# Wide loads, 128-key tiles, planned dates and zero matmuls in a fused attention and MLP kernel

## The chip, the cores and the metric

The kernel runs on one core of one Trainium2 chip. The metric is the device time of one execution in microseconds (us); a median of several executions is given, with the lowest and highest. A profile is one such execution. Its span is from the first to the last recorded instruction. PE is TensorE, PEld its weight loads, ACT ScalarE, DVE VectorE, POOL GpSimd, SP SyncE.

## The reference

Attention over 8 batches of 12 heads, 448 tokens and 64 channels, with root-mean-square normalised q and k, followed by an MLP with a hard swish between its two products.

```python
q, k, v: (8, 12, 448, 64)   g_q, g_k: (64,)   w_in: (768, 2048)   w_out: (2048, 768)

q_n = q / sqrt(mean(q * q, -1) + 1e-6) * g_q          # k_n likewise
attn = softmax(q_n @ k_n.T / sqrt(64))
x = (attn @ v).transpose(0, 2, 1, 3).reshape(8 * 448, 768)
h = x @ w_in
out = (h * clip(h + 3, 0, 6) / 6) @ w_out              # (3584, 768), float32
```

## The kernel before

The work goes by pairs of heads: 6 pairs per batch, 48 in all. A pair of k and q is loaded, squared, reduced, scaled and turned (its channels brought onto the partitions). Scores are then computed with the keys on the partitions, in four tiles of 112 keys, and go through an exponential. The value matmuls follow; v carries a column of ones, which gives the softmax's denominator. The normalised rows are turned again into `xT`, and the MLP of a batch can start when all six pairs of it are in `xT`. The MLP of batch b runs interleaved with the attention of batch b+1, so PE is full once batch 0 is done; before that it has only batch 0's attention to do. The kernel describes all work as steps with durations and due times, and a small greedy planner fixes each engine's order before the program is built.

```python
T = 4; PT = S // T                                   # 112 partitions, 4 tokens in each
def load_g():                                        # four loads of single elements, on ScalarE's queue
    for a in range(2):
        nc.scalar.dma_start(out=gq_t[a * 64:(a + 1) * 64, :], in_=g_q.rearrange("(p o) -> p o", o=1))
        nc.scalar.dma_start(out=gk_t[a * 64:(a + 1) * 64, :], in_=g_k.rearrange("(p o) -> p o", o=1))
# ... cut ...
def score(t0=t0, taken=taken):                       # attend(P): a tile of 112 keys, two heads
    for i, (ps, _, _) in enumerate(taken):
        for a in range(2):
            rows, c0 = slice(a * 64, a * 64 + 64), (t0 + i) * PT
            nc.tensor.matmul(out=ps[:, a, 0:S], lhsT=kp[rows, c0:c0 + 128],
                             rhs=kq[rows, 1, :], start=True, stop=True)
# ... one exponential of 112x896 per tile, then the values:
def values(dst, c0, first):
    for a in range(2):
        for t in range(T):
            nc.tensor.matmul(out=dst[:, a * E1:(a + 1) * E1], lhsT=e[0:PT, t, a, c0:c0 + 128],
                             rhs=va[0:PT, a, t, :], start=(first and a == 0 and t == 0), stop=(t == T - 1))
# ... cut ...
NPE = 10                                             # pairs whose q and k are turned by PE, the rest by DMA
def weights(c, at, load, kept):                      # 8 weight loads, issued by GpSimd between its other work
    kept[c] = add("POOL", 0.9, at, lambda: load(c), gate, xfer=4.4, after=at)
# ... cut ...
with tc.manual_schedule():
    for s in plan.order():
        s.fn(s.eng)
```

Of the kernel before, what the change touches and what calls it, by code (L numbers as in the profile page):

```python
# [15 lines left out]
RELU = mybir.ActivationFunctionType.Relu  # L16
AX_X = mybir.AxisListType.X
PSUM = bass.MemoryType.PSUM

# [13 lines left out]

class Plan:
# [3 lines left out]

    LAT = {"PE": 0.20, "ACT": 0.18, "DVE": 0.15, "POOL": 0.20, "SP": 0.0}
    DMA_LATENCY = 1.7  # L40
    SOFT, HARD = 0.64, 0.425
    AHEAD, HURRY = 0.0, 6.0

    def __init__(self):
        self.steps = []

    def add(self, on, dur, due, fn, *deps, xfer=0.0, after=0.0, lock=False, late=0.0):
        on, f = ({on: dur}, lambda e: fn()) if isinstance(on, str) else (on, fn)
        s = Step(on, due, f, deps, xfer, after, lock, late, len(self.steps))
        self.steps.append(s)  # L50
        return s

    def hard(self, soft, at, todo):

        for t0, t1 in soft:
            if t1 <= at:
                continue
            part = min(todo, max(0.0, t0 - at))
            at, todo = at + part, todo - part
            if todo <= 0:  # L60
                return at
            part = min(todo, (t1 - at) * self.HARD)
            at, todo = at + part / self.HARD, todo - part
            if todo <= 0:
                return at
        return at + todo

    def order(self):
        users = {id(s): [] for s in self.steps}
        left = {}  # L70
        for s in self.steps:
            left[id(s)] = len(s.deps)
            for d in s.deps:
                users[id(d)].append(s)
        free = dict.fromkeys(self.LAT, 0.0)
        port = dma_free = dma_soft = 0.0
        soft = []
# [3 lines left out]
        def release(s):  # L81
            for e in s.on:
                ready[id(s), e] = max([s.after] + [
                    d.end + (0.06 if d.eng == e and not d.xfer else self.LAT[d.eng]) for d in s.deps])
                open_[e].append(s)

# [4 lines left out]
        while len(done) < len(self.steps):  # L91
            best = None
            for e, l in open_.items():
                for s in l:
                    at = max(free[e], ready[id(s), e], port if s.lock and e in ("DVE", "POOL") else 0.0)
                    if best is None or at < best[0]:
                        best = (at, e)
            assert best is not None, "steps wait for each other"
            at, e = best
            near = []  # L100
            for s in open_[e]:
                t = max(at, ready[id(s), e], port if s.lock and e in ("DVE", "POOL") else 0.0)
                if t <= at + self.AHEAD:
                    near.append((s.due + self.HURRY * (t - at), s.n, t, s))
            _, _, at, s = min(near)
# [3 lines left out]
            free[e] = s.end = at + s.on[e]  # L109
            if s.lock and e in ("DVE", "POOL"):  # L110
                port = s.end
            if s.xfer:
                if e == "POOL":
                    at = max(dma_soft, s.end)
                    dma_soft = at + s.xfer / self.SOFT
                    soft.append((at, dma_soft))
                    s.end = dma_soft + self.DMA_LATENCY
                else:
                    dma_free = self.hard(soft, max(dma_free, s.end), s.xfer)
                    s.end = dma_free + self.DMA_LATENCY + s.late  # L120
            done.append(s)
            for u in users[id(s)]:
                left[id(u)] -= 1
                if not left[id(u)]:
                    release(u)
# [3 lines left out]
class Ring:  # L129


    def __init__(self, bufs):
        self.bufs = bufs
        self.used = [[] for _ in bufs]
        self.i = -1

    def take(self):
        self.i += 1
        k = self.i % len(self.bufs)
        before, self.used[k] = self.used[k], []  # L140
        return self.bufs[k], before, self.used[k]
# [3 lines left out]
def kernel(  # L145
# [16 lines left out]
    T = 4  # L162
# [7 lines left out]
    NP = B * NJ  # L170
    assert PT == 112 and S - SM == 64 and D == 64 and NKT == NJ and B % 2 == 0
# [7 lines left out]
    gq_t, gk_t, gp = (const.tile([128, 1], FP32, name=n) for n in ("gq_t", "gk_t", "gp"))  # L179
    mark = const.tile([1, 1], FP32, name="mark")  # L180
    ident = const.tile([128, 128], BF16, name="ident")
    w_in_sb = const.tile([128, NKT, DFF], BF16, name="w_in_sb")
    w_out_sb = const.tile([128, NFT, DM], BF16, name="w_out_sb")

    qk_r = Ring(tiles("qk", 5, [128, 2, 2, T * D], FP32))
    vf_r = Ring(tiles("vf", 5, [128, 2, T * D], FP32))
    sq_r = Ring(tiles("sq", 2, [128, 2, 2, T * D], FP32))
    ssq_r = Ring(tiles("ssq", 4, [128, 4 * T], FP32))
    rs_r = Ring(tiles("rs", 4, [128, 4 * T], FP32))
    qks_r = Ring(tiles("qks", 3, [128, 2, T, 2, D]))  # L190
    kq_r = Ring(tiles("kq", 4, [128, 2, S]))
    kp_r = Ring(tiles("kp", 3, [128, S + 16]))
    va_r = Ring(tiles("va", 5, [128, 2, T, E1]))
    e_r = Ring(tiles("e", 3, [128, T, 2, S]))
    xn_r = Ring(tiles("xn", 3, [128, NS, 2, D]))
    rd_r = Ring(tiles("rd", 3, [128, NS, 2], FP32))
# [6 lines left out]
    X_r = Ring(tiles("X", 1, [128, 512], FP32, psum))  # L203
    R_r = Ring(tiles("R", 1, [128, 512], FP32, psum))
    M_r = Ring(tiles("M", 2, [128, 512], FP32, psum))

    plan = Plan()
    add = plan.add

    NPE = 10  # L210
    GATE, W_IN_AT, W_OUT_AT, W_STEP = 2, 7.0, 35.0, 6.3
    START, FIRST, PAIR = 9.0, 4.1, 2.3
    LEAD = 4
    HURRY = 0.8
# [27 lines left out]
    for P in range(NP):  # L242
        b = P // NJ
        begin.append(begin[-1] + (FIRST if b == 0 else (
            sum(x[3] for x in seq[b]) / NJ + PAIR + (1.1 if (P + 2) < NPE else 0.0))))
    begin += [begin[-1] + 8.0 * (i + 1) for i in range(8)]

# [4 lines left out]
    def load_g():  # L252
        for a in range(2):
            nc.scalar.dma_start(out=gq_t[a * 64:(a + 1) * 64, :], in_=g_q.rearrange("(p o) -> p o", o=1))
            nc.scalar.dma_start(out=gk_t[a * 64:(a + 1) * 64, :], in_=g_k.rearrange("(p o) -> p o", o=1))
# [7 lines left out]
    def make_ones():  # L263
        for t in va_r.bufs:
            nc.gpsimd.memset(t[:, :, :, D:E1], 1.0)
        for t in kp_r.bufs:
            nc.gpsimd.memset(t[:, S:S + 16], 0.0)

    g_load = add("ACT", 2.2, 0, load_g, after=1.5, late=3.0)
    g_make = add("DVE", 0.1, 0, lambda: nc.vector.scalar_tensor_tensor(  # L270
        out=gp[:], in0=gq_t[:], scalar=8.0, in1=gk_t[:], op0=MULT, op1=MULT), g_load, after=7.5)
    id_make = add("POOL", 0.5, 0, make_ident)
    one_make = add("POOL", 0.6, 0, make_ones)

    def load_w_in(c):
        n = DFF // 4
        nc.gpsimd.dma_start(
# [3 lines left out]
    def load_w_out(c):  # L281
        cols, f0 = slice((c // 2) * HALF, (c // 2 + 1) * HALF), (c % 2) * (NFT // 2)
        nc.gpsimd.dma_start(
# [5 lines left out]
    L, V, SC, KQ = {}, {}, {}, {}  # L289

    def heads(src, P):
        b, j = divmod(P, NJ)
        return src[b, 2 * j:2 * j + 2, :, :].rearrange("h (p t) d -> p h (t d)", t=T)

    def loads(P):
        at = begin[P]
        qk, war, use = qk_r.take()
        res = []
# [375 lines left out]
```

## Time and profile before

| kernel before | |
|---|---|
| time | 443.15 us (442.05 to 443.25, 3 runs) |
| span and time of the profiled execution | 438.6 us, 440.47 us |
| first square, first score, first MLP matmul | 8.89, 14.28, 45.48 us |
| PE busy | 410.6 us, 94% |
| exponentials on ScalarE | 166.3 us |

Two lines of the page's groups show what the change goes for. The columns are: source line, engine, operation, out<-in, shapes and count; then busy us and mean ns of one; then the engine's idle time before them and what ended it.

```profile
L421 ACT ACTIVATE e<-S 112x896 bf16<-112x896 f32 x192 | 166.3, 914 | 64.1 <-PE S L416 64.0
L359 POOL CAST va<-vf 112x512 bf16<-112x512 f32 x48 | 31.5, 658 | 10.4 <-DMA vf<-in_v_dram 10.1
```

The exponential takes 914 ns for 896 columns on 112 of 128 partitions.

One caution: the profiled execution of before was a fast one. The time of most others was 442 to 443 us, 2 us above it. Profiles are therefore used to find where time goes, and the medians to say how much.

### The profile page before, as it was taken

Reading aid. Unit: us, or ns where it says so; the run is one execution under the profiler, and the core shown is the slowest. Engines: PE = TensorE matmul, PEld = TensorE weight load, DVE = VectorE, ACT = ScalarE, POOL = GpSimd, SP = SyncE. Lnnn points to the kernel's source line nnn. Section 1 sums busy time; section 2 is a strip of 40 time slices with the busy share of each in tenths; the row PEclk is TensorE's granted clock in tenths of the full one; section 3 lists DMA queues with packets and bytes.
Section 4 is the critical chain, followed back from the end, with each engine's and each line's share of the span. In section 5 each row is a group of like instructions: output and inputs, shape, how many; then the busy total and the mean of one; then the engine's idle time right before and its main releaser. Section 6 shows DMA issues by size and latency. Waiting matters only on the chain.

```text
span 438.6 us, 9205 instructions
## 1 busy us (share of the span) xinstructions
PE 410.6 (94%) x3663; PEld 229.2 (52%) x3682; DVE 246.3 (56%) x417; ACT 249.0 (57%) x425; POOL 240.2 (55%) x230
## 2 busy tenths in 40 slices
PE   0588799999999999999999999999999999999995
PEld 0355455555455565554455565554455555654563
DVE  1998887657674564456555465556564444334421
ACT  3788588657765666367664677357673665123200
POOL 3499988855757567656765657747757510000000
PEclk9999999999999999999999999999999999999999
DMA  8999999877545745674465655684465420220122
GB/s 241 247 265 261 224 214 193 216 197 192 128 121 148 189 113 136 167 214 111 133 156 157 177 135 145 159 214 109 120 161 164 97 56 12 54 81 0 37 72 73
DMA packets 102923, 64.58 MB, mean 147 GB/s; under 512 B 59744, under 2 KB 99424, under 8 KB 102880
## 3 DMA queue, kind: packets, MB, share of 16 engines
q1 hardware_dynamic: 94544, 57.01, 50.6%
q0 software_dynamic: 7296, 6.29, 9.1%
q10 hardware_dynamic: 1040, 0.69, 0.5%
q8 instruction: 29, 0.48, 0.5%
q14 instruction: 14, 0.11, 0.1%
HBM read 45.61 MB, written 11.01 MB: 129 GB/s over the span
## 4 chain that ended last, share of the span: by engine, by line
PE 80%; POOL 5%; DVE 4%; ACT 3%; issue 3%; DMA 3%; SPq 1%; POOLq 0%
PE M L558 27%; PE M L533 25%; PE S L416 9%; PE X L437 8%; PE S L558 4%; PE R L437 2%; PE S L533 2%; DVE ssq L337 1%; ACT e L421 1%; POOL qks L351 1%; PE X L558 1%; POOL sq L322 1%; POOL va L359 1%; DMA gq_t<-in_g_q_dram 1%; POOL sq L329 1%
## 5 line engine op out<-in xcount | busy, mean ns | idle before, releaser
L421 ACT ACTIVATE e<-S 112x896 bf16<-112x896 f32 x192 | 166.3, 914 | 64.1 <-PE S L416 64.0
L533 PE MATMUL M<-xT,w_in_sb 128*128 128x384 bf16 (+1 forms) x679 | 145.1, 349 | 3.7 <-DVE gT L541 2.9
L351 POOL TENSOR_TENSOR qks<-qk,rs 112x512 bf16<-112x512 f32 x87 | 90.5, 1055 | 86.6 <-ACT rs L344 84.7
L558 PE MATMUL M<-w_out_sb,gT 128*128 128x384 bf16 x736 | 131.8, 326 | 0.0
L558 PEld LDWEIGHTS <-gT 128*128 128x128 bf16 x896 | 82.9, 98 | 57.8 <-issue 7.8
L533 PEld LDWEIGHTS <-w_in_sb 128*128 128x128 bf16 x768 | 69.6, 97 | 67.4 <-issue 12.5
L541 DVE SCALAR_TENSOR_TENSOR gT<-t,M 128x384 bf16<-128x384 f32 (+1 forms) x116 | 70.6, 611 | 59.1 <-ACT t L539 58.3
L539 ACT ACTIVATE t<-M 128x384 f32<-128x384 f32 (+1 forms) x116 | 62.6, 540 | 67.0 <-PE M L533 65.5
L437 PEld LDWEIGHTS <-e 112*128 112x128 bf16 x1536 | 65.1, 99 | 31.4 <-issue 16.0
L337 DVE TENSOR_REDUCE ssq<-sq 112x16 f32<-112x1024 f32 (+1 forms) x49 | 58.4, 1193 | 23.3 <-POOL sq L329 12.2
L329 POOL TENSOR_TENSOR sq<-qk 112x1024 f32<-112x1024 f32 x36 | 68.1, 1892 | 0.0
L416 PE MATMUL S<-kq,kp 64*128 64x448 bf16 x384 | 56.6, 364 | 4.1 <-DVE kp L381 1.7
L437 PE MATMUL X<-va,e 112*128 112x65 bf16 x1152 | 58.6, 196 | 0.8 <-ACT e L421 0.6
L566 DVE COPY y<-M 128x384 f32<-128x384 f32 x46 | 25.6, 556 | 59.2 <-PE M L558 59.0
L359 POOL CAST va<-vf 112x512 bf16<-112x512 f32 x48 | 31.5, 658 | 10.4 <-DMA vf<-in_v_dram 10.1
L392 POOL TENSOR_SCALAR kp<-kq,gp 128x448 bf16<-128x448 bf16 x23 | 32.3, 1402 | 5.3 <-DMA kq<-qks 5.2
L463 DVE TENSOR_TENSOR xn<-X,rd 128x384 bf16<-128x384 f32 x48 | 26.8, 558 | 1.6
L416 PEld LDWEIGHTS <-kp 64*128 64x128 bf16 x384 | 12.2, 94 | 27.7 <-issue 18.0
L437 PE MATMUL R<-va,e 112*128 112x65 bf16 x384 | 20.4, 195 | 0.0
L377 PE MATMUL M<-ident,qks 112*128 112x112 bf16 x80 | 7.9, 242 | 13.0 <-DVE qks L351 12.4
L558 PE MATMUL S<-w_out_sb,gT 128*128 128x384 bf16 x112 | 19.5, 326 | 0.0
L462 DVE RECIPROCAL rd<-X 128x6 f32<-128x6 f32 x48 | 9.2, 192 | 15.3 <-PE X L437 15.2
(42 smaller groups left out, 156.2 us busy)
## 6 DMA issues: line engine op xcount, KB each, us to landing
qk<-in_k_dram SPq DMA_DIRECT2D x48, 224.0 KB, 3.3
vf<-in_v_dram SPq DMA_DIRECT2D x48, 224.0 KB, 3.7
qk<-in_q_dram SPq DMA_DIRECT2D x45, 224.0 KB, 3.4
w_in_sb<-in_moe_w_in_dram POOLq DMA_DIRECT2D x4, 768.0 KB, 11.3
w_out_sb<-in_moe_w_out_dram POOLq DMA_DIRECT2D x4, 768.0 KB, 11.9
out_dram<-y SPq DMA_DIRECT2D x8, 336.0 KB, 3.1
out_dram<-y SPq DMA_DIRECT2D x8, 288.0 KB, 3.4
out_dram<-y SPq DMA_DIRECT2D x8, 240.0 KB, 3.2
```

Of the source, the lines that this page charges most:

```text
L329: parts = [add("POOL", 1.93, at - 10, lambda: nc.gpsimd.tensor_tensor(out=sq[0:PT], in0=qk[0:PT], in1=qk[0:PT], op=MULT), *ld, *war, lock= ...
L337: red = add("DVE", 0.6 * n, at - 8 * hurry + 0.5 * i0, lambda i0=i0, i1=i1, cs=cs: nc.vector.tensor_reduce(out=ssq[0:PT, cs], in_=sq[0:PT, ...
L351: sc.append(add(on, 0, at - 6 * hurry, lambda e, i=i, rs4=rs4: engines[e].tensor_tensor(out=qks[0:PT, i].rearrange("p t h d -> p h t d"), ...
L359: vc = add({"POOL": 0.61}, 0, at - 3, lambda e: engines[e].tensor_copy(out=va[0:PT, :, :, 0:D], in_=vf[0:PT].rearrange("p h (t d) -> p h t ...
L392: nc.vector if e == "DVE" else nc.gpsimd).tensor_scalar_mul(
L416: nc.tensor.matmul(out=ps[:, a, 0:S], lhsT=kp[rows, c0:c0 + 128], rhs=kq[rows, 1, :], start=True, stop=True)
L421: x = add("ACT", 0.93, at + step * (t0 + i) / T + 0.2, lambda t=t0 + i, ps=ps: nc.scalar.activation(out=e[0:PT, t], in_=ps[0:PT, :, 0:S], ...
L437: nc.tensor.matmul(out=dst[:, a * E1:(a + 1) * E1], lhsT=e[0:PT, t, a, c0:c0 + 128], rhs=va[0:PT, a, t, :], start=(first and a == 0 and t ...
L533: nc.tensor.matmul(out=m[:, 0:n], lhsT=w_in_sb[:, kt, f * 128:(f + 1) * 128], rhs=X[:, kt, :], start=(kt == 0), stop=(kt == NKT - 1))
L539: r = add("ACT", 0.08 + n / 1200, due + span, lambda: nc.scalar.activation(out=t[:, 0:n], in_=m[:, 0:n], func=RELU, bias=0.5, scale=1.0 / ...
L541: g = add("DVE", 0.12 + n / 960, due + span, lambda: nc.vector.scalar_tensor_tensor(out=G[:, f, :], in0=t[:, 0:n], scalar=1.0, in1=m[:, 0: ...
L558: nc.tensor.matmul(out=m[:, 0:HALF], lhsT=G[:, f, i * 128:(i + 1) * 128], rhs=w_out_sb[:, f, cols], start=(f == 0), stop=(f == NFT - 1))
```

## The change

Its intent: fewer and fuller instructions for attention, an earlier start, and an order of work that was tuned against a finer model of the engines and DMA queues.

1. Keys in three tiles of 128 and a rest of 64, in place of four of 112. The rests of two heads share one matmul (a block-diagonal weight), those of two pairs one exponential.
2. For batches 0 and 1: loads with 7 tokens on each of 128 partitions ("wide"), q, k and x turned by PE, v cast by GpSimd or ScalarE.
3. g in two row loads, turned by PE; k and q are no longer issued by ScalarE.
4. Three tables, by step number: shifts of due dates (`NUDGES`), fixed engines (`ENGINES`), earliest starts (`HOLD`); and a planner with a model of DMA queues and a backward pass.
5. Explicit waits of GpSimd for VectorE, where the plan marks an operation of each as using the port that they share (see the prediction, "What the skill says").
6. Matmuls of zeros where the plan shows PE idle, up to 115 us. They add zero to parts of the accumulators X and S.

The diff at its core (cuts are marked):

```diff
+NUDGES = {9: -3332, 10: -1597, 11: -472, ... cut: 208 entries ...}
+ENGINES = {46: "ACT", 50: "POOL", 55: "POOL", ... cut: 47 entries ...}
+HOLD = {37: 39, 39: 33, 41: 31, 42: 1, ... cut: 149 entries ...}
+    def load_wide(at, tile_, src, P, war, after):
+        return [add("SP", 0.43, at, lambda: nc.sync.dma_start(
+            out=tile_[:, 0:U].rearrange("p t d -> p (t d)"),
+            in_=heads(src, P).rearrange("h (p t) d -> (h p) (t d)", t=U)), *war, xfer=(8, 1950), after=after)]
... cut ...
-            nc.scalar.dma_start(out=gq_t[a * 64:(a + 1) * 64, :], in_=g_q.rearrange("(p o) -> p o", o=1))
-            nc.scalar.dma_start(out=gk_t[a * 64:(a + 1) * 64, :], in_=g_k.rearrange("(p o) -> p o", o=1))
+        return nc.scalar.dma_start(
+            out=grow[:, i].rearrange("o (a p) -> o a p", a=2), in_=(g_q, g_k)[i]... cut ...)
... cut: scores ...
+                    if t < NS:
+                        for a in range(2):
+                            fns.append(... nc.tensor.matmul(
+                                out=ps[:, a, 0:S], lhsT=kp[a * 64:a * 64 + 64, t * 128:(t + 1) * 128],
+                                rhs=rhs[a], start=True, stop=True))
+                    else:
+                        fns.append(... nc.tensor.matmul(
+                            out=ps[:, slot, 0:S], lhsT=kb[:, P % NJ], rhs=rhs[2], start=True, stop=True))
... cut ...
+    order = plan.order()
+    def fill(t0, t1):
+        while t1 - t0 > 0.1:
+            for t, l in reads:                       # l: when the plan has others reading this tile
+                if not any(x - 0.05 < t0 < y + 0.2 for x, y in l):
+                    n = t.shape[-1]
+                    nc.tensor.matmul(out=t, lhsT=zero[:, 0:128], rhs=zero[:, 0:n], start=False, stop=False,
+                                     skip_group_check=True)
+                    t0 += n / 1200 if t0 < COLD else n / 2400 / FILL
+                    break
+            else:
+                t0 += 0.1
     with tc.manual_schedule():
-        for s in plan.order():
-            s.fn(s.eng)
+        for s in order:
+            if s.eng == "PE":
+                if s.start < FILL_TO and s.start - free > 0.3:
+                    fill(free, s.start - 0.1)
+                free = s.end
+            ins = s.fn(s.eng)
+            if ins is not None and s.lock and s.eng in ("DVE", "POOL"):
+                if s.eng == "POOL" and holder is not None:
+                    tc.add_manual_dep(ins.ins, holder.ins.name, ... cut ..., reason="port")
+                holder = ins if s.eng == "DVE" else None
```

## The prediction

> **What bounds the kernel now.** I read the granted clock first (1.000 on the one core, so nothing is throttled), then the busy times, then the slices, then the same per stage, then the waits and the timeline. Busy time of the engines:
>
> ```profile
> PE 410.6 (94%) x3663; PEld 229.2 (52%) x3682; DVE 246.3 (56%) x417; ACT 249.0 (57%) x425; POOL 240.2 (55%) x230
> PE   0588799999999999999999999999999999999995
> DMA  8999999877545745674465655684465420220122
> ```
>
> TensorE is busy nearly throughout, except in the first six or so slices of 11 us. There the DMA row is at its fullest. By stage (busy us of PE, weight loads, VectorE, ScalarE, GpSimd; clock; DMA share; GB/s):
>
> ```profile
> 0.00:14.00 14.00, 1.11 (x8) 0.65 (x9) 4.29 (x8) 5.57 (x13) 3.70 (x19) 1.00 0.94 233
> 14.00:45.50 31.50, 25.11 (x315) 14.94 (x316) 29.18 (x50) 24.74 (x40) 27.48 (x29) 1.00 1.16 262
> 45.50:60.00 14.50, 12.49 (x140) 7.81 (x140) 12.32 (x21) 9.50 (x21) 13.95 (x16) 1.00 1.23 216
> 60.00:380.00 320.00, 317.76 (x2901) 176.31 (x2918) 181.02 (x309) 199.62 (x337) 195.01 (x169) 1.00 0.59 147
> 380.00:434.30 54.30, 54.10 (x307) 29.45 (x307) 18.95 (x32) 9.55 (x16) 0.00 (x0) 1.00 0.18 51
> ```
>
> So there are three regimes: a start up to 60 us, in which VectorE (29.2 of 31.5 us) and GpSimd (27.5) are full and PE is not; a long stage in which PE sets the pace; and 54 us of pure matmuls at the end. What delays the start, from the waits and the chain of waits:
>
> ```profile
> ACT sq L320 <- DMA gq_t<-in_g_q_dram: 6.9, 1, 6.9
> PE M L377 <- DVE qks L351: 12.4, 3, 11.7
> 16.24 2.48 DVE sq L322
> 34.37 0.83 POOL w_in_sb L277
> 36.52 0.80 issue
> 37.31 1.03 POOL qks L351
> 38.34 1.02 POOL va L359
> 39.36 0.89 POOL w_out_sb L283
> ```
>
> The first k is in at 4.2 us, but ScalarE is issuing four tiny loads of g until 8.9 us, so the first square starts at 8.89, the first transpose at 11.7, the first score at 14.3. From 33 to 54 us the chain lies mostly on GpSimd, which scales q and k, casts v and issues weight loads in between. The first MLP matmul runs at 45.5 us.
>
> **PE's price list.** Busy times of matmuls overlap, so I took start-to-start times of back-to-back runs from the timeline: six 384-column matmuls 0.98 us (0.163 each), six of 512 columns 1.295, four score matmuls (64x448, two heads) 0.49, eight of 65 columns 0.26, eight key/query transposes 0.4 to 0.5. The sum: MLP 64x0.98 + 64x1.295 + 896x0.163 = 291; a pair of heads costs 2x0.49 + 4x0.26 = 2.02, times 48 = 97; transposes for 10 pairs 5; x of batch 0 about 1. That is 394 us of work in 434.3. Of the 40 us idle, about 30 lie before 60 us (work done there: 50 MLP matmuls 8, scores 8, values 9, transposes 5), some 10 are small gaps in the long stage, such as 0.48 us where 0.26 would do.
>
> **What the skill says.** "TensorEngine Tiling (Array Packing)", Tiling Modes, lists two row tiles of 64x128. The trace agrees: 448 columns cost 122 ns per score matmul (0.49/4), less than a 384-column full-height one (163 ns), so the two heads run side by side. "TensorE: Matmul & The Clock Gate", Part 1, says the array starts at half rate and is released after about 3.4 us of sustained work. The trace agrees: a score pair takes 0.55 us until 24 us and 0.36 from 26 us on, four transposes 0.55 then 0.37, at a granted clock of 1.000. "GPSIMD Engine Reference", Specifications, says GpSimd's SBUF interfaces are shared with VectorE and contend when VectorE reads two SBUF inputs. The trace agrees: the same square takes VectorE 0.68 to 2.55 us while GpSimd works beside it. "DMA: Bandwidth & Descriptors", Specifications, asks for at least 512 B per transfer for line rate; the rests of 64 keys are loaded as 256 B rows, which no run yet shows.
>
> **The change, part by part.**
> 1. *128-key tiles.* 448 keys were 4x112; now 3x128 and a rest of 64. Values: four groups of 6 instead of 8, 4x0.20 = 0.80 us instead of 1.04; the rest adds 8 matmuls of 64 rows, two heads side by side, at 33 ns each and 4 turns about 0.13. Scores: over two pairs, four clusters of 0.49 become three, and one of two full-height 448-column matmuls (the rests of both heads by a block-diagonal weight), 2x0.19 = 0.38. Sum over two pairs: before 4.04, after 3x0.49 + 0.38 + 2x0.93 = 3.71; 0.33 less, times 24 = **8 us of PE**. All of it after 60 us (21 of 24) is on the path.
> 2. *Exponentials.* 4 per pair become 3.5: 192x0.914 = 166 us of ScalarE becomes about 154 (the rests of batch 0 are done singly, at about 0.5). Off the path later, useful in the start.
> 3. *Wide loads and PE turns for batches 0 and 1.* 128 partitions with 7 tokens rather than 112 with 8: squares, reductions and scales shrink to 0.875 (VectorE's reduction 1.21 to about 1.06, GpSimd's scale 1.05 to 0.92), the cast of v 0.63 to about 0.5 and now possibly on ScalarE. Two more pairs are turned by PE (2x0.45), and x of batch 1 also (6x0.2): **2 to 2.5 us more PE**, in exchange for DMA transposes that take 2.3 to 3.3 us to land in the busiest DMA stretch.
> 4. *g.* Two loads of a row instead of four of single elements, k and q no longer issued by ScalarE: the first square can start at about 4.5 rather than 8.9. **4 to 5 us** earlier for the first pair.
> 5. *Explicit waits for the shared port, choice of engine, dates and holds.* These don't remove work. They remove stretching (2.55 back to 0.68) and put weights at better moments.
> 6. *Zero matmuls.* They fill PE's gaps up to 115 us, so each cold operation is about 0.2 us shorter in the first 24 us. They are in gaps, and PE is in order: where the real timing runs ahead of the table they delay real work by little: 240 columns are about 0.1 us warm and 0.2 cold, by the prices above.
> 7. *Added:* loads and preparation of the key rests per batch, small copies (0.25 us per pair), a rest normalisation per pair (0.29) instead of one per three (0.76). VectorE's sum hardly moves; it has room after 60 us (181 of 320).
>
> **The start, summed.** One pair of batch 0 costs the three vector engines together about 11.0 us now (ScalarE 3.7 exponentials + 0.4 + squares 1.2; VectorE 1.2, 0.7, 0.45, 0.38, 0.75, 0.25, 0.35; GpSimd 1.05, 0.6) and about 10.3 after: 3.7 against 3.4 us per pair if spread evenly. Now batch 0 takes 31 us from first score to first MLP matmul, over 5 per pair, so most is stretching and waiting. I take 4.5 per pair after, and a first score at 9: 9 + 27 = 36 us for the first MLP matmul, 9 or 10 us earlier. DMA allows it: six pairs (6x0.67 MB) and w_in (3.1 MB as counted at the destination) are 7.1 MB, 28 us at the 250 GB/s seen. Some is given back in the hot stretch after it, so I count **9 us**.
>
> **Sum.** 8 - 2.3 on PE, 9 from the start, and 4 of the 10 us of small gaps through the finer order: 443.15 - 5.7 - 9 - 4 = 424.45. I put 423, since rival (d) below reaches further down from here than it costs to miss.
>
> **Rivals.** *(a) DMA holds the start.* Its share is above 0.9 up to 60 us; all weights and 12 pairs are 14.4 MB, 58 us at 250 GB/s, and the change adds 256 B pieces. Then H starts no sooner than about 42 and only PE's work and some gaps are gained: 432 to 434. For it: the full DMA row. Against: GpSimd and VectorE, not DMA, carry the chain from 9 to 54 us. *(b) The tables fit a model and not the chip.* The many fixed dates make waits where reality is late: gaps of the long stage stay or grow, 428 to 440. *(c) Another engine becomes the bound.* ScalarE has 200 of 320 us and loses 12; GpSimd has 195, plus explicit waits. I don't believe it. *(d) Everything fits:* H at 33 us and gaps nearly gone, 414 to 417. The floor: PE work 388, 8 us before it can begin, 4.3 for the last store, 4.5 between profiled span and measured time, and at least 10 us idle in batch 0, about 415.
>
> **Range and chances.** From (d) to the better half of (a) and (b): 413 to 434. A gain under 2% needs 434.3 or more, which takes both the start and the gaps to fail: 9%. Slower by 2% would take a new stall in the long stage: 2%.
>
> **What would show it.** First square at 4.5 us, first score at 9, first MLP matmul near 36; ScalarE's exponentials near 154 us; two score clusters and one rest cluster per 3.7 us of attention work; PE full from about 50 us; the last 54 us unchanged. The prediction is wrong if the rest matmuls don't run side by side (0.27 instead of 0.13 a pair: 7 us lost), if DMA holds H beyond 42 us, or if the gaps in the long stage stay.

## The result and the profile after

The changed kernel took **436.99 us** (434.78 to 438.37, 4 runs) against 442.68 us (442.05 to 443.25, 4 runs) for the kernel before. The ratio is 0.987, with a 95% interval of 0.982 to 0.991; a second set of rounds (the control run below) gave 0.989. Ratios here are the mean time of one kernel's runs over the mean of the other's of the same rounds, so they are not quite the ratio of the medians. That is a gain of 1.3% and lies above the predicted range of 413 to 434 us. The result is correct.

Busy time of the engines, then three rows of the slices (40 slices of 10.9 us; tenths of busy share, and tenths of the full clock), from the page of the changed kernel:

```profile
PE 417.5 (96%) x4057; PEld 244.9 (56%) x4057; DVE 241.4 (55%) x472; ACT 249.8 (57%) x454; POOL 210.1 (48%) x270
PE   7858899999999999999999999999999999999995
PEclk9978999999999999999999999999999999999999
DMA  8999998669877846697657787485564320310122
```

PE is busier, and yet the time fell: part of the busy time is zeros. New are the third and fourth slices of the clock row (22 to 44 us), which show 7 and 8 tenths; before it showed 9s throughout. In the third slice PE's row has a dip to 5. Three of the stages of before (us of the stage; busy us of PE, weight loads, VectorE, ScalarE, GpSimd; granted clock, DMA share, GB/s):

```profile
0.00:14.00 14.00, 10.73 (x119) 7.26 (x120) 8.95 (x18) 9.34 (x19) 8.90 (x28) 1.00 0.90 228
14.00:45.50 31.50, 23.50 (x402) 16.52 (x401) 19.28 (x45) 21.59 (x43) 17.97 (x23) 0.84 1.16 243
60.00:380.00 320.00, 318.45 (x3069) 184.49 (x3068) 188.75 (x371) 192.72 (x342) 174.96 (x211) 1.00 0.65 149
```

From 14 to 45.5 us VectorE, ScalarE and GpSimd have 19.3, 21.6 and 18.0 us of work, against 29.2, 24.7 and 27.5 before. Most of the stretching is gone (VectorE's squares in the first 60 us take 0.61 to 0.63 us, before up to 2.55), and no engine is full. Even so, that stage does not end sooner. The first score starts at 9.44 us (before 14.28) and the first MLP matmul at 50.32 us (before 45.48). These are their rows in PE's timeline (start, duration, engine, line, operation, out<-in, shapes, count; in brackets the idle time before it and what ended it):

```profile
9.44 0.55 PE L801 MATMUL S<-kq,kp 64*128 64x448 bf16 x4 [0.28 <-ACT kq L522]
50.32 1.95 PE L969 MATMUL M<-xT,w_in_sb 128*128 128x384 bf16 x11
```

So a lead of 4.8 us at the first score has become a lag of 4.8 us at the first MLP matmul. From that matmul to the end of the span it is 435.8 - 50.3 = 385.5 us, before 438.6 - 45.5 = 393.1: the long stage is 7.6 us shorter. The sum, -7.6 + 4.8 = -2.8, is what the two spans differ by; the medians differ by 5.7, as the profiled execution of before was 2 us faster than most of its kind and that of after 1.4 us slower than its median.

PE's waits in the first 60 us (what waited, what for, us in total, times, longest):

```profile
PE X L890 <- POOL va L524: 4.1, 1, 4.1
PE X L1112 <- DVE xn L909: 2.5, 2, 1.6
PE X L1112 <- DVE X L1122: 2.2, 1, 2.2
PE X L1112 <- DVE xr L913: 0.8, 1, 0.8
PE S L801 <- ACT e L834: 0.7, 2, 0.5
```

Two things are new. A value matmul (L890) waits 4.1 us for a cast of v. And three of the five rows are of the zero matmuls (L1112): work that is there to fill gaps waits itself, 3.3 us for VectorE to read X (xn, xr) and 2.2 us for X's first zeroing (L1122). GpSimd's timeline shows what held the cast (start, us; in brackets the idle time before it and what ended it):

```profile
26.83 0.95 POOL L524 CAST va<-vf 128x384 bf16<-128x384 f32 x2 [5.30 <-DMA vf<-in_v_dram]
28.16 0.93 POOL L560 TENSOR_TENSOR sq<-kf 128x448 f32<-128x448 f32 x1 [0.39 <-DMA kf<-in_k_dram]
```

In GpSimd's order, the first of the two casts is that of the sixth pair, and its v landed at 26.7 us. The second is that of the second pair, whose v had long been there; PE was waiting for this one. The kernel's own plan, which can be printed when the kernel is built, has the sixth pair's cast at 21.8 us. GpSimd was idle for 5.3 us because the planned order, which the tables shape, put a cast with late data ahead of a cast with ready data. The granted clock over these microseconds, in stages of 5 us with the columns as above:

```profile
20.00:25.00 5.00, 3.38 (x74) 2.43 (x71) 3.72 (x10) 3.37 (x8) 1.53 (x2) 1.00 1.18 246
25.00:30.00 5.00, 2.17 (x36) 1.69 (x37) 0.62 (x2) 1.09 (x4) 2.39 (x4) 0.63 1.18 244
30.00:35.00 5.00, 5.00 (x80) 3.25 (x77) 3.84 (x10) 3.20 (x6) 3.18 (x4) 0.50 1.17 270
35.00:40.00 5.00, 3.84 (x67) 2.50 (x64) 3.27 (x9) 4.15 (x10) 2.66 (x3) 0.84 1.17 248
```

PE paused from 23.7 to 27.8 us. In stages of 1 us the clock reads 1.00 or 0.50, but for the two in which it changes. So it is either full or half here; a mean of 0.63 puts the fall at 26.3 us, and 0.84 puts the return at 36.6 us: ten microseconds at half clock. In the third row PE is busy for all of 5 us, at half its speed.

Three groups of the page, with the columns explained above:

```profile
L834 ACT ACTIVATE e<-S 128x896 bf16<-128x896 f32 x144 | 124.8, 914 | 32.0 <-PE S L801 31.6
L834 ACT ACTIVATE er<-S 128x896 bf16<-128x896 f32 (+1 forms) x27 | 22.5, 832 | 8.6 <-PE S L806 8.4
L1112 PE MATMUL X<-zero 128*128 128x240 bf16 x98 | 15.2, 290 | 5.9 <-DVE xn L909 2.5 <-DVE X L1122 2.2 <-DVE xr L913 1.3
```

The exponentials come to 124.8 + 22.5 = 147.3 us, 19 us less than before at the same 914 ns each. The 98 zero matmuls into X take 15.2 us of PE (overlapping), and 50 more go into S.

### The profile page after: what moved, and what is told of

Read it like the earlier page. It is cut to its first block, busy times and chain, and to the rows that moved or that the text cites. A ratio compares the mean times of both kernels' runs of the same rounds, so it can differ in the third digit from the quotient of the medians.

```text
span 435.8 us, 10149 instructions
## 1 busy us (share of the span) xinstructions
PE 417.5 (96%) x4057; PEld 244.9 (56%) x4057; DVE 241.4 (55%) x472; ACT 249.8 (57%) x454; POOL 210.1 (48%) x270
## 4 chain that ended last, share of the span: by engine, by line
PE 87%; DMA 4%; DVE 4%; ACT 1%; issue 1%; SPq 1%; POOL 0%; DVEq 0%; ACTq 0%; POOLq 0%
PE M L969 28%; PE M L994 28%; PE X L890 9%; PE S L801 7%; PE S L994 4%; PE S L969 2%; DMA vf<-in_v_dram 2%; PE X L994 2%; PE S L806 2%; PE X L772 1%; DMA kf<-in_k_dram 1%; PE X L969 1%; PE M L653 1%; DVE ssq L577 1%; DMA qf<-in_q_dram 1%
## 5 line engine op out<-in xcount | busy, mean ns | idle before, releaser
L834 ACT ACTIVATE e<-S 128x896 bf16<-128x896 f32 x144 | 124.8, 914 | 32.0 <-PE S L801 31.6
L890 PE MATMUL X<-va,e 128*128 128x65 bf16 x1152 | 51.6, 196 | 4.5 <-POOL va L524 4.1
L890 PEld LDWEIGHTS <-e 128*128 128x128 bf16 x1152 | 45.5, 99 | 17.6 <-issue 9.1
L577 DVE TENSOR_REDUCE ssq<-sq 128x14 f32<-128x896 f32 (+1 forms) x49 | 51.7, 1060 | 6.1 <-POOL sq L560 4.1
L560 POOL TENSOR_TENSOR sq<-qf 112x512 f32<-112x512 f32 (+1 forms) x38 | 39.2, 1034 | 21.1 <-DVE kp L675 7.7
L600 POOL TENSOR_TENSOR qks<-kf,rs 128x384 bf16<-128x384 f32 x36 | 29.8, 829 | 29.9 <-ACT rs L584 24.7
L560 POOL TENSOR_TENSOR sq<-kf 128x384 f32<-128x384 f32 (+1 forms) x40 | 33.4, 837 | 19.7 <-DVE kp L675 8.1
L609 POOL TENSOR_TENSOR qks<-qf,rs 112x512 bf16<-112x512 f32 x36 | 37.6, 1045 | 7.3 <-ACT rs L584 5.6
L524 POOL CAST va<-vf 128x384 bf16<-128x384 f32 x46 | 23.1, 506 | 32.6 <-PE X L890 15.7
L909 DVE TENSOR_TENSOR xn<-X,rd 128x384 bf16<-128x384 f32 x48 | 26.7, 557 | 1.7
L834 ACT ACTIVATE er<-S 128x896 bf16<-128x896 f32 (+1 forms) x27 | 22.5, 832 | 8.6 <-PE S L806 8.4
L1112 PE MATMUL X<-zero 128*128 128x240 bf16 x98 | 15.2, 290 | 5.9 <-DVE xn L909 2.5
```

The costliest lines, as they stand in the source:

```text
L524: return (nc.vector if e == "DVE" else nc.gpsimd).tensor_copy(out=out, in_=x)
L560: return engines[e].tensor_tensor(out=o, in0=x, in1=x, op=MULT)
L577: lambda i0=i0, i1=i1, rows=rows: nc.vector.tensor_reduce(out=ssq[0:rows, i0:i1], in_=sq[0:rows, i0:i1], axis=AX_X, op=ADD),
L600: return engines[e].tensor_tensor(out=qks[:, 0:NS].rearrange("p t (h d) -> p h t d", h=2), in0=kf[:, 0:KH].rearrange("p (h t) d -> p h t d ...
L609: return engines[e].tensor_tensor(out=qks[0:PT, NS:QB].rearrange("p t (h d) -> p h t d", h=2), in0=qf[0:PT].rearrange("p (h t) d -> p h t ...
L834: lambda dst=dst, ps=ps, w=2 if whole else 1: nc.scalar.activation(out=dst, in_=ps[:, 0:w, 0:S], func=EXP), s, *(AVW[P] if t < NS else AVR ...
```

## The experiments

Eighteen kernels were run, each with 5 rounds against the kernel before. The runs of one call share a chip, those of different calls don't, so between calls the ratios compare better than the medians. "First MLP" is the start of the first MLP matmul in the profiled execution, and "rest" the span from there to its end. A profile is one execution and scatters by some 2 us, so small differences in the last two columns mean little.

| kernel | median (range), us | ratio to before, 95% | first MLP, us | rest, us |
|---|---|---|---|---|
| control: the changed kernel again | 437.5 (435.2-438.7) | 0.989 (.986-.992) | 50.1 | 385.5 |
| 1 sixth pair's cast later | 436.9 (435.3-438.7) | 0.987 (.985-.990) | 47.8 | 385.4 |
| 2 stall filled with zeros | 434.9 (434.7-436.0) | 0.983 (.982-.985) | 47.5 | 385.5 |
| 3 no zero matmuls | 433.0 (431.6-434.4) | 0.979 (.977-.981) | 45.2 | 384.6 |
| 4 no tables | 441.5 (441.3-441.8) | 0.998 (.997-.999) | 46.1 | 393.9 |
| 5 zeros only up to 20 us | 433.1 (431.9-434.7) | 0.977 (.974-.980) | 47.8 | 384.6 |
| 6 no zeros, cast later | 432.3 (431.4-434.3) | 0.976 (.972-.979) | 45.8 | 384.6 |
| 7 as 6, weights later | 432.3 (431.4-433.8) | 0.975 (.972-.978) | 47.2 | 384.8 |
| 8 no zeros, few weights (wrong result) | 430.5 (429.8-433.0) | 0.972 (.969-.975) | 43.5 | 384.5 |
| 9 no zeros, no port waits | 433.3 (431.9-433.7) | 0.979 (.976-.981) | 46.6 | 385.0 |
| 10 before, g and issues alone | 445.5 (444.5-447.4) | 1.007 (1.005-1.010) | 44.3 | 399.2 |
| 11 before, few weights (wrong result) | 442.6 (441.8-443.6) | 1.001 (.998-1.003) | 46.3 | 394.8 |
| 12 zeros only into S | 438.1 (437.8-438.7) | 0.991 (.988-.993) | 51.1 | 384.9 |
| 13 no zeros, batch 1 prepared later | 437.5 (436.7-439.1) | 0.990 (.987-.993) | 45.6 | 389.5 |
| 15 all three: 3, 1 and 13 | 437.6 (435.1-438.5) | 0.989 (.986-.992) | 46.6 | 389.5 |
| 16 as 3, six exponentials left out (wrong) | 432.4 (431.0-434.7) | 0.980 (.977-.983) | 43.4 | 385.9 |
| 17 as 8, six exponentials left out (wrong) | 430.8 (429.8-432.3) | 0.976 (.973-.978) | 45.8 | 384.7 |
| 18 as 6, stall filled with zeros | 432.7 (432.4-433.1) | 0.980 (.978-.982) | 46.0 | 384.6 |

One reading before the details: in all kernels with the tables, whose later work is left in place, the rest is 384.5 to 385.9 us. A microsecond of the first MLP matmul is a microsecond of the time. The question is therefore what sets the first MLP matmul.

### 1 and 2: the stall at 24 us

Theory A: the sixth pair's cast stands ahead of the second's, and its late v stalls GpSimd, then PE, and the pause then brings half clock. Run 1 only moves that cast behind the casts of pairs two to four in GpSimd's order. Run 2 leaves the stall and puts 34 zero matmuls ahead of the value matmuls that wait, so that PE is kept busy and the clock should stay up.

```diff
 order = plan.order()
+order.remove(CAST[5])                                # run 1
+order.insert(order.index(CAST[2]) + 1, CAST[5])
```

```diff
 free = s.end
+if s is stall:                                       # run 2: the PE step that waits for the second pair's cast
+    for _ in range(34):
+        nc.tensor.matmul(out=idle[0][2], lhsT=zero[:, 0:128], rhs=zero[:, 0:240], start=False, stop=False, ...)
```

> Only the place of one GpSimd instruction changes: the cast of the sixth pair's v goes behind the casts of the second to fourth pairs. Theory A (queue order: the cast that waits for a late load stands in front of one whose data is long there, PE waits 4.1 us for it and its clock then falls to half): the stall at 23.7 us and the half clock from 27 to 36 us vanish, the first MLP matmul comes at 43 to 46 us instead of 50.3, the time falls by 3 to 6 us. Theory B (the DMA engines hold the start whatever the order): another wait for a load takes its place, the first MLP matmul stays at 48 to 50 us, the time within 1 us of the changed kernel's.

> The stall stays, but 34 more zero matmuls (some 3.5 us) stand in front of the matmuls that wait, so that PE does not fall idle. Theory A with the half clock as its main harm: the granted clock stays at 1.00 from 25 to 40 us, the first MLP matmul comes 2 to 4 us earlier, the time falls by 1 to 3 us. If the stall itself is the harm: the clock stays up but the first MLP matmul moves by less than 1 us, the time by less than 1 us.

Run 1 took 436.9 us, the same as the changed kernel. The clock stayed full from 20 to 30 us (and fell to 0.66 from 30 to 35), but PE still waited once for a cast: a square whose k landed late stands in GpSimd's order too, and stalled it in the same way.

```profile
PE X L891 <- POOL va L524: 2.8, 1, 2.8
```

Moving one step of a queue mends one wait, and the next late load makes another. Run 2 took 434.9 us with a clock of 1.00 from 20 to 45 us: in this kernel the half clock costs about 2 us. The start still took until 47.5 us. So theory A has the stall right, and explains 2 of some 14 us.

### 3, 5 and 12: what the zero matmuls do

Run 3 sets the end of filling to 0, so that there are none. Run 5 sets it to 20 us. Run 12 lets zeros go only into S, never into X.

```diff
-    FILL, FILL_FROM, FILL_TO, COLD = 0.7, 1.2, 115.0, 6.0
+    FILL, FILL_FROM, FILL_TO, COLD = 0.7, 1.2, 0.0, 6.0     # run 3; run 5 has 20.0
```

```diff
-    idle = [(X_r, 0, X_r.bufs[0][:, 1, 272:512]), (S_r, 0, S_r.bufs[0][:, 0, S:512]),
+    idle = [(S_r, 0, S_r.bufs[0][:, 0, S:512]),             # run 12
             (S_r, 1, S_r.bufs[1][:, 0, S:512])]
```

> No zero matmuls at all. If they keep PE quick as intended: the first scores take 0.55 instead of 0.36 us, more half clock before 50 us, the time 1 to 3 us longer. If they stand in the way of real work, or PE's speed there does not matter since other engines and loads hold the start: the time is the same within 1 us or 1 to 2 us shorter.

> Zero matmuls only up to 20 us of the plan, where they warm PE, none after. If their harm is in the later ones, which stand in PE's queue ahead of real work and wait for VectorE to finish reading X: as fast as without any (433.0 us) or 1 us faster, first scores at 0.36 us each. If the early ones do harm as well: 435 to 437 us.

> Zero matmuls as in the changed kernel but only into the two S tiles, never into X. If they harm since they wait for VectorE to finish reading X and hold up the real matmuls behind them: 433 to 434.5 us, and the first MLP matmul at 45 to 47 us. If their place in PE's order does the harm: 435.5 to 437.5 us as in the changed kernel.

Without zero matmuls the time is 433.0 us: **they cost 4 us** instead of saving any. The first MLP matmul came at 45.2 us, five earlier. Run 5 is as fast as run 3 (433.1), so those of the first 20 us do no harm and no good, and the later ones do the harm. They did make PE quick at first: without them the first four score matmuls took 0.93 us in place of 0.55 (the recorded clock reads 1.00 in both, so it doesn't show this), and the first score still started at 9.3 us.

Run 12 was meant to free PE from waiting for X's readers, and took 438.1 us. Its waits and stages:

```profile
PE S L1112 <- ACT e L834: 5.7, 6, 1.6
PE S L1112 <- DVE S L1122: 3.2, 1, 3.2
PE S L1112 <- ACT er L834: 1.2, 3, 0.6
```

```profile
15.00:20.00 5.00, 3.47 (x55) 2.62 (x55) 1.95 (x4) 2.92 (x6) 2.69 (x4) 0.50 1.11 208
20.00:25.00 5.00, 4.50 (x73) 3.20 (x70) 1.98 (x5) 1.92 (x5) 2.27 (x3) 0.50 1.17 243
25.00:30.00 5.00, 3.99 (x62) 2.91 (x61) 2.22 (x5) 2.41 (x6) 2.73 (x4) 0.50 1.18 244
```

Now they wait for the exponentials that read S. A zero matmul writes to a tile that others read, so it waits for those reads like any other matmul. The `fill` function looks up in the plan when the tile is free, but where the chip is later than the plan, the zero matmul waits for a reader and the real matmul behind it waits too. And the short zeros (64 columns) with their waits did not hold the clock: it was at 0.50 from 15 to 30 us.

### 4: are the tables worth anything

```diff
-    plan = Plan(NUDGES, ENGINES, HOLD)
+    plan = Plan({}, {}, {})
```

> The three tables are empty, the order is what the kernel's own planning gives. If the tables fit the chip: 3 to 10 us slower than the changed kernel, with more gaps on PE after 60 us. If they fit only the plan (rival b of the prediction): within 2 us of the changed kernel, or faster, and no stall on the sixth pair's cast at 23.7 us.

Without tables, 441.5 us. The first MLP matmul is then 4 us earlier than in the changed kernel (46.1), but the long stage takes 393.9 us in place of 385.5. In the stage from 60 to 380 us PE is busy 314.8 us, against 318.5 with the tables:

```profile
60.00:380.00 320.00, 314.84 (x3033) 181.14 (x3034) 182.26 (x355) 191.29 (x340) 179.40 (x213) 1.00 0.69 148
```

The tables earn about 8 us in the long stage and lose about 4 in the start. Without them PE doesn't wait for a cast of v in the first 60 us. So they fit the chip in the long stage (DMA share 0.65 there) and not in the start (above 1); that late loads make the difference is argued, no run isolates it.

### 6, 7 and 8: do the loads hold the start

Run 6 joins 3 and 1. Run 7 also moves two of the weight loads (the second and the fourth of `w_in`) behind casts. Run 8 is run 3 with only a quarter of the weights loaded and used, so that the DMA share falls from 30 us on. If the loads of weights hold the start, run 8 must be much faster.

```diff
-        kept[c] = add("POOL", 0.9, at, lambda: load(c), gate, xfer=(48, size), after=at, lock=True)
+        kept[c] = add("POOL", 0.9, at, lambda: load(c) if c == 0 else None, gate, ...)   # run 8; the matmuls reuse these weights
```

```diff
+order.remove(W_in[1])                                # run 7, on top of run 6
+order.insert(order.index(CAST[5]) + 1, W_in[1])
+order.remove(W_in[3])
+order.insert(order.index(W_in[1]) + 1, W_in[3])
```

> No zero matmuls, and the sixth pair's cast behind those of the second to fourth pairs. Queue order: PE's 1.6 us wait for a cast that is left without zero matmuls goes, time 1 to 2 us below 433.0. Loads hold the start: within 0.7 us of 433.0.

> As the run before, and the second and third loads of w_in, issued at 14 and 17 us, come behind the casts, at about 25 us. If the weights take the DMA engines from batch 0's loads: k, q and v land sooner, the first MLP matmul comes at 40 to 43 us and the time falls 2 to 4 us below that of the run before, unless w_out then comes late, which would show as PE waiting for it near 75 us. If compute holds batch 0: the first MLP matmul moves by less than 1 us.

> Wrong result on purpose: only one of four parts of w_in and of w_out is loaded and used for all (4.7 of 6.3 MB at the destination are gone), no zero matmuls, everything else in the same order. If the DMA engines hold the start (rival a of the prediction): the first MLP matmul comes at 36 to 40 instead of 45 us and the time falls by 5 to 9 us from 433.0. If VectorE, GpSimd and ScalarE or their order hold it: it comes at 43 to 45 us and the time falls by less than 2 us.

Run 6 took 432.3 us, the best correct version, within the scatter of run 3. Run 7 gained nothing over it. Run 8 took 430.5 us with the first MLP matmul at 43.5:

```profile
30.00:40.00 10.00, 6.81 (x159) 4.93 (x156) 7.99 (x21) 9.20 (x19) 4.15 (x5) 1.00 0.49 127
```

The DMA share is 0.49 from 30 to 40 us there (1.18 in run 3), at full clock, and all of it is worth 2.5 us. The weights are a small part of the miss. The run says less of the loads of q, k and v, which it leaves: from 5 to 30 us the DMA share is still 1.05 to 1.14, GpSimd stands idle for 2.4 us until the sixth pair's v lands, and two loads lie in the chain that ends at the first MLP matmul (start, us; then the cast in GpSimd's timeline):

```profile
8.44 5.48 DMA kf<-in_k_dram
16.62 7.49 DMA vf<-in_v_dram
24.24 0.95 POOL L524 CAST va<-vf 128x384 bf16<-128x384 f32 x2 [2.40 <-DMA vf<-in_v_dram]
```

No run thinned those loads.

### 9: the explicit port waits

```diff
-                if s.eng == "POOL" and holder is not None:
+                if False:                            # on top of run 3
```

> No zero matmuls, and GpSimd no longer waits explicitly for VectorE's last operation on the shared port; the order is the same. If these waits only move the cost from stretched operations to waiting: within 1 us of the 433.0 without zero matmuls, and single operations of VectorE and GpSimd stretched again (a square on VectorE over 0.8 us, GpSimd's scale over 1.1). If they gain what they were meant to: 1 to 3 us slower.

433.3 us, the same as run 3. The operations did become longer. This is the same group, first in run 3 and then in run 9, in the first 60 us:

```profile
L560 DVE TENSOR_TENSOR sq<-qf 128x448 f32<-128x448 f32 x3 | 1.9, 618 | 0.0
```

```profile
L560 DVE TENSOR_TENSOR sq<-qf 128x448 f32<-128x448 f32 x3 | 2.3, 764 | 0.0
```

VectorE's square goes from 618 to 764 ns where GpSimd may work beside it. Taking turns costs the same time as sharing, so the waits gain nothing here and cost nothing.

### 10 and 11: parts of the change in the kernel before

Run 10 takes one part alone into the kernel before: k and q are issued by SyncE and ScalarE loads g first, so that the first square needn't wait. Run 11 loads a quarter of the weights in the kernel before, by the edit of run 8.

```diff
-            e = "ACT" if i and P < 3 else "SP"
+            e = "SP"
-    g_load = add("ACT", 2.2, 0, load_g, after=1.5, late=3.0)
+    g_load = add("ACT", 2.2, -20, load_g, after=0.7, late=3.0)
```

> The kernel before, with one part of the change alone: q of the first three pairs is loaded by SyncE's queue and g is issued by ScalarE at once, so that ScalarE is free when k lands. As predicted (4 to 5 us earlier for the first pair, of which the path keeps most): first square at 4.5, first score near 10, the first MLP matmul 2 to 4 us earlier and the time 2 to 4 us shorter. If the vector engines' work sets the pace of batch 0: first score near 10, first MLP matmul and time within 1 us.

> Wrong result on purpose: the kernel before with a quarter of the weights loaded. If the DMA engines hold its start: the first MLP matmul at 36 to 40 us instead of 45.5, 5 to 9 us shorter. If GpSimd and VectorE hold it: 44 us or later, less than 2 us shorter apart from the 6 issues of GpSimd that are gone (0.9 us each).

Run 10 has its first square at 3.4 us (5.5 earlier) and its first score at 10.4 (3.9 earlier), and is **3 us slower** than before (445.5). Its first MLP matmul comes at 44.3 us, then PE waits again:

```profile
48.61 2.40 PE L533 MATMUL M<-xT,w_in_sb 128*128 128x384 bf16 x7 [3.38 <-DVE xT L480]
```

A lead at the first score is not a lead at the sixth pair: it was still 4.3 us at the first pair's normalisation (18.98 us) and 0.7 at the sixth's (43.46). Run 11 (442.6 us) shows that the loads of weights don't hold the start of the kernel before either.

### 13 and 15: does batch 1's preparation hold batch 0

In the changed kernel, ten pairs are prepared before the first MLP matmul (eight before), so I suspected that VectorE's and GpSimd's work for batch 1 stands in batch 0's way. Run 13 moves the preparation of the ninth to eleventh pairs behind the first MLP matmul, without zeros; run 15 adds run 1's move.

```diff
+    h0 = H_last[0][0]
+    early = [s for s in order[:order.index(h0)] if s in PREP[8] + PREP[9] + PREP[10]]
+    for s in early:
+        order.remove(s)
+    order[order.index(h0) + 1:order.index(h0) + 1] = early
```

> No zero matmuls, and the preparation (squares, sums, scales) of the ninth to eleventh pairs, of which nine operations stand before the first MLP matmul in the engines' queues, comes right behind it. If the work for batch 1 is what holds the first MLP matmul: it comes 2 to 3.5 us earlier than the 45.2 us without zero matmuls. The time then falls by as much if VectorE and ScalarE have room afterwards (430 to 431.5), or stays at 433 if they have not. If latencies of batch 0's own chain hold it: less than 1 us earlier, time 432.5 to 434.

> No zero matmuls, the sixth pair's cast behind the others, and the late preparation: if the gains add, 1 us below the run r13; if they are the same time found twice, within 0.7 us of it.

They took 437.5 and 437.6 us, slower than run 3 by 4.5. The first MLP matmul did not come earlier (45.6 against 45.2), and the delayed preparation then stood in the way of the MLP's own VectorE work:

```profile
PE M L971 <- DVE gT L979: 3.6, 1, 3.6
```

That theory fell: batch 1's preparation fits into holes of batch 0's chain.

### 16 and 17: does ScalarE hold batch 0

In run 8 ScalarE is busy 30 of the 35 us from 9 to 44 us, so it was the last single engine to suspect. Runs 16 and 17 leave out the middle one of the three full exponentials of each pair of batch 0 (6 x 0.914 = 5.5 us of ScalarE), on top of runs 3 and 8, with everything else in the same order.

```diff
-  lambda dst=dst, ps=ps, ...: nc.scalar.activation(out=dst, in_=ps[:, 0:w, 0:S], func=EXP)
+  lambda dst=dst, ps=ps, ..., go=not (P < NJ and t == 1): nc.scalar.activation(...) if go else None
-  out=X[...], lhsT=e[:, t, a, c0:c0 + 128], rhs=va[:, a * NS + t, :],
+  out=X[...], lhsT=e[:, 0 if P < NJ and t == 1 else t, a, c0:c0 + 128], rhs=va[:, a * NS + t, :],
```

> Wrong result on purpose: the changed kernel without zero matmuls (433.0 us, first MLP matmul at 45.2 us), and of the three full exponentials of each pair of batch 0 the middle one is left out (six in all, 0.914 us each, 5.5 us of ScalarE); TensorE and the others do the same work in the same order. Theory A, ScalarE is what batch 0's chain is bound by (it is busy 30 of 35 us of it, with copies and squares that the tables gave it): the first MLP matmul moves forward by 4 to 5.5 us, to 40 to 41 us, and the time falls to 428 to 429 us. Theory B, the bound is the order in which TensorE, VectorE and ScalarE wait for one another, or the loads: less than 1.5 us, 431.5 to 433 us.

> Wrong result on purpose: the same six exponentials left out, and only a quarter of the weights loaded (that alone: 430.5 us, first MLP matmul at 43.5 us). Theory A, ScalarE binds once the loads are light: 38 to 39.5 us for the first MLP matmul, 425 to 426.5 us. Theory B, neither ScalarE nor the loads but the order of the engines: 42 to 43.5 us, 429 to 430.5 us. If this one moves by 4 us and the other does not, ScalarE and the loads hold the start side by side.

432.4 and 430.8 us: 0.6 us less and 0.3 more than the same kernels with these exponentials, and by the ratios to before of their own rounds no less at all (0.980 and 0.976 against 0.979 and 0.972). In run 16's profile the first MLP matmul is 1.8 us earlier, less than half of what theory A asked for; run 17's profiled execution happened to fall to a clock of 0.84 from 20 to 30 us, and its 45.8 us is no evidence either way. These exponentials are not the bound, nor are they together with the loads of weights.

### 18 and the control

Run 18 puts 20 zero matmuls only at the stall of the best version, by the edits of runs 6 and 2; the control is the changed kernel once more.

> The fastest version so far (no zero matmuls, sixth pair's cast behind the casts of pairs two to four: 432.3 us, first MLP matmul at 45.8, a granted clock of 0.66 from 30 to 40 us) with 20 zero matmuls, about 2 us, put only ahead of the value matmuls that wait 2.0 us for the cast. If the half clock costs what it seemed to (about 2 us): 430 to 431 us with a clock of 1.00. If the time of the start is set elsewhere: 432 to 433 us.

> The changed kernel as it is, a control on the same chip as its neighbours: 435 to 438 us, first MLP matmul at 48 to 50.5 us, the wait for the cast of 4 us seen again, and 3 to 5 us slower than the run without zero matmuls in the same call.

Run 18 took 432.7 us with a clock of 0.997, so a fuller clock gained nothing here: in the best version the half clock is not what holds the start. The control gave 437.5 us and a ratio of 0.989, so the main result stands. The best correct version is run 6, at 432.3 us (ratio 0.976), faster than before by 2.4% and than the changed kernel by 1.1%.

## Why the prediction was wrong

**Right in kind: the long stage.** The prediction had two pairs of attention at 3.71 us of PE after against 4.04 before. By start-to-start times in the trace of the changed kernel it is 3.66: a score cluster of four 0.48, or 0.60 with rest values behind it, a rest cluster 0.38, values 0.20 for each group of six (2x0.60 + 0.48 + 0.38 + 8x0.20). The turns for batches 0 and 1 cost more than predicted (0.56 us for 28 matmuls, not 0.45). The rest from the first MLP matmul to the end fell by 7.6 us, where the prediction had 9.7 (5.7 of PE work and 4 of gaps). By these prices some 6 of the 7.6 are PE work, which leaves 1.6 for gaps; this split is an estimate. By it, the step "4 of the 10 us of small gaps" was 2.4 us too high.

**Right: the first steps of the start.** First square predicted at 4.5 and measured at 3.39; first score predicted at 9 and measured at 9.44. Exponentials predicted at 154 us, measured at 147.3; 3.5 of 4 of the 166 us are 146, so the 154 was a slip in the sum. GpSimd and VectorE stretch less. Two readings were too quick: "so nothing is throttled" (at that recorded clock of 1.000 a score pair took 0.55 us until 24 us and 0.36 later, as the prediction says itself), and 4.5 us between span and time, which compares two executions (in one it was 440.47 - 438.6 = 1.9).

**Wrong: the step "The start, summed".** It counted six pairs at 4.5 us each from the first score and arrived at 36 us for the first MLP matmul. It came at 50.3. The difference of 14.3 us is about the whole miss: with 36, the profiled execution would have taken about 438.4 - 14.3 = 424.1. The starts of the pairs' normalisations (`xn`, on VectorE) show which term of the sum failed. These are those of the first and of the sixth pair, in the kernel before, the changed kernel and run 3:

```profile
23.29 0.56 DVE L463 TENSOR_TENSOR xn<-X,rd 128x384 bf16<-128x384 f32 x1
44.11 0.56 DVE L463 TENSOR_TENSOR xn<-X,rd 128x384 bf16<-128x384 f32 x1
```

```profile
21.78 0.56 DVE L909 TENSOR_TENSOR xn<-X,rd 128x384 bf16<-128x384 f32 x1
48.21 0.56 DVE L909 TENSOR_TENSOR xn<-X,rd 128x384 bf16<-128x384 f32 x1
```

```profile
22.91 0.56 DVE L909 TENSOR_TENSOR xn<-X,rd 128x384 bf16<-128x384 f32 x1
43.70 0.56 DVE L909 TENSOR_TENSOR xn<-X,rd 128x384 bf16<-128x384 f32 x1
```

| us | first score | from there to the first pair's `xn` | each further pair, to the sixth's `xn` | from there to the first MLP matmul | first MLP matmul |
|---|---|---|---|---|---|
| predicted | 9 | 4.5, as any pair | 4.5 | none | 36 |
| before | 14.3 | 9.0 | 4.2 | 1.4 | 45.5 |
| changed kernel | 9.4 | 12.3 | 5.3 | 2.1 | 50.3 |
| run 3: no zeros | 9.3 | 13.6 | 4.2 | 1.5 | 45.2 |
| run 8: no zeros, few weights | 9.5 | 13.6 | 3.8 | 1.5 | 43.5 |

- **The first pair: 7.8 us of the miss, 9.1 without zeros.** The sum gave it 4.5 us from first score to normalisation. It took 12.3 in the changed kernel and 13.6 in runs 3 and 8. Before it was 9.0, so a measured number stood in the profile, hidden in the average of "over 5 per pair". The lead of 4.8 us at the first score was down to 1.5 us at the first normalisation (21.8 against 23.3), and to 0.4 in run 3. In run 3 the first pair's three full exponentials were done at 12.4 us, but its rest scores came at 18.1 and its values at 19.6: in PE's order the second pair's scores and the third pair's turns stand between. So the first pair is late partly because work for the next pairs was done meanwhile. Whether another order would gain, no run tried.
- **The pace after it** was not too low a guess: without zeros it is 4.2 us per pair (3.8 with few weights), under the predicted 4.5.
- **The zero matmuls: 5 us** (the changed kernel against run 3; 4 in the medians). They bring the first normalisation forward by 1.1 us and lose 6.2 after it; of this loss the half clock after the 4.1 us stall is about 2 (run 2). In part 6 I wrote that they "delay real work by little: 240 columns are about 0.1 us warm". The price of one was right; what I left out was that they wait, 3.3 us in the trace, for the readers of the tile that they write, with real work behind them.
- **The loads of weights: 1.7 us** (run 3 against run 8; 2.5 in the medians). Rival (a), "DMA holds the start", is small as far as weights go, and untested for the loads of q, k and v (see run 8). Its figures, 432 to 434 us and a first MLP matmul not before 42, are what the kernel without zeros shows (433.0 and 45.2); whether for its reason is open.

Runs 13, 15, 16 and 17 exclude that batch 1's preparation or the middle exponentials alone are the bound. That the engines wait for one another in turn, with one X and two M accumulators and fixed orders, is argued and not shown. So the step that failed is known; what makes the first pair long stays open.

**Rival (b)**, "the tables fit a model and not the chip", was half right. I expected it in the long stage, and it happened in the start: the plan has the sixth pair's cast at 21.8 us, where the chip, whose v came late, did it at 26.8. In the long stage the tables earn about 8 us (run 4). The same plan has the first MLP matmul at about 42 us and its last step ending at 433, so reading it would have warned against 36 and 423.

**Wrong part of the chances.** I held a gain under 2% to need both the start and the gaps to fail, at 9%. The start alone could fail by 14 us, more than the range allowed.

## What to carry to other kernels

A chain of overlapping pairs has a length for its first pair and a pace for the rest. Read both from the profile as it is (here 9.0 us, then 4.2 per pair), since one average over all pairs hides the first; and lower either only where you can name the wait that goes. A lead at the head is not a lead at the end. A filler instruction on an in-order engine should write where no other engine reads, or it waits and holds the real work behind it (no run here had such a place). A planned order on an in-order queue should not put a step with late data ahead of one whose data is there, and a table tuned on a model should be checked on the chip where the loads are fullest.

## What the Trainium skill lacked or had wrong

- "TensorE: Matmul & The Clock Gate", Part 1, gives about 3.4 us both for release to the full rate and for falling back. The fall came somewhat sooner (2.6 us into a pause of 4.1 us, as worked out from the clock's means). The release took longer: in the changed kernel PE was at work again from 27.8 us and busy for all of 30 to 35 us, and was released at about 36.6 us, after some 9 us. In run 12 PE was busy 4.50 of 5 us from 20 to 25 us and stayed at 0.50.
- No page that I read warns that zero matmuls for warmth wait for the readers of the tile they write: 3.3 us of such waits in the first 60 us of the changed kernel and 6.9 in run 12; the time is 4 us less when all zero matmuls go.
- "GPSIMD Engine Reference", Specifications, tells of the SBUF interfaces shared with VectorE. It doesn't say what avoiding the contention is worth in a kernel: VectorE's square went from 0.62 to 0.76 us without the waits (run 9), and the kernel's time did not change (433.3 and 433.0 us).
